# Attention beside an MLP: when sums are cleared, how many scores a phase has, and which banks they use

## The chip, the cores and the metric

The kernel runs on one core of a Trainium2 chip. The metric is the device time of one execution in microseconds (us). Before the change three runs took 1433.83, 1438.09 and 1441.65 us; the median is 1438.09 us.

## The reference

```
g = sigmoid((x * gate_w).sum(-1))
a = softmax_attention(x)            # 32 heads of 16, scores q.k * 16**-0.5, then @ wo
b = mixer(x)                        # w2^T gelu(w1^T layernorm(x) + b1) + b2, over the tokens
out = g * a + (1 - g) * b
```

x is 2048 tokens by 512 channels, w1 is 2048 x 1792, w2 is 1792 x 2048. Everything is float32; the kernel splits operands into a high and a low part and multiplies three times.

## The kernel before, in words

First come the projections to q, k and v and the first layer of the mixer (up to about 304 us). Everything after that is one schedule, written out by hand, of **phases**. A phase issues 8, 12 or 14 score matmuls; among the first of them it issues as many matmuls of other work (**beside** work), then the matmuls that multiply finished exponentials with v, then the additions. Two phases with the same beside work are a **double**: every beside matmul is split in two halves of 64 rows, one for each phase of the double, and both add to the same bank (`dn`). So that the halves never overlap, POOL writes a one-element `token` (L1152) after the last beside matmul of a phase, and the first beside matmul of the next phase (L1146) waits for it.

**Units, groups, slots, banks.** A score matmul (L990) gives one **unit**: 128 keys by 512 queries of one head, in one of seven PSUM banks. A **group** is a pair of heads with half of the queries: 64 units; there are 32 groups, 2048 units. Most units are exponentiated by ACT straight from the bank (L1020), one, two or three neighbouring banks in one instruction. Some are copied by DVE to SBUF first (L1140) and exponentiated there by ACT at the start of the next phase (L1034); now and then DVE does a whole one with a polynomial (L1046 to L1059). Every result takes a **slot** of 128x512 in SBUF: 25 in `arena` and 4 in `more`, given back when v's matmuls (L938) have read it. `matched` pairs the finished units of a group; `apply_v` multiplies them, to a bank that the phase's table names (`av_bank`, and `other_bank` for a second group); `add_sums` (L961) lets DVE add that bank to the group's sums `ot`.

The table `TURN` has, for each size of phase, the bank of every score, the scores that ACT takes together, the scores that DVE copies, and the two banks for v. For twelve:

```
12: [((0, 1, 4, 5, 6, 2, 3, 0, 1, 4, 5, 6), ((0,), (2,), (4,), (6,), (7, 8, 5), (9, 10, 11)), (1, 3), 3, 2)]
```

**Ends of groups.** When a group is complete, `store_sums` queues five transfers on SP (L884, L886), and `open_sums` of the group after next allocates `ot` (two buffers) and clears it on POOL (L874). At the end of a group's scores SP also gets 14 loads for the group after next (L515). POOL, SP, PE, ACT and DVE each run their instructions in the order in which they were queued.

**Stages.** The beside work of the first 61 doubles is the mixer's second layer (16 tiles of 42 matmuls, three doubles of 12 scores and one of 14 per tile). Then two doubles, of 14 and 8 scores, carry none; `open_end` gives the mixer's buffers to the output stage there and the four slots of `more` and one of `arena` are closed (`room`). Then 22 doubles of eight scores carry the output projection of token tiles 0 to 7 (12 matmuls each): their input comes as eight transfers a tile (`fetch_tile`, L743, L744) and is divided on DVE (L712). The last eight doubles, of eight scores, carry 8 of 12 matmuls for tiles 8 to 15; `fetch_o` (L720, L721) brings whole blocks for these. A tail finishes.

Of the kernel before, what the change touches and what calls it, by code (L numbers as in the profile page):

```python
# [10 lines left out]
F32 = mybir.dt.float32  # L11
# [11 lines left out]
P = 128  # L23
S = 2048
D = 512
# [50 lines left out]
def gated_mix(ctx: ExitStack, tc: tile.TileContext, a_x, a_wqkv, a_wo, b_w1, b_b1, b_w2, b_b2, gate_w, out):  # L76
# [3 lines left out]
    def split(hi, lo, src, copy, sub):  # L80

        copy(hi, src)  # L82
        return sub(lo, src, hi.bitcast(F32), ALU.subtract)  # L83
# [444 lines left out]
    def second_out(t, ps):  # L528
# [21 lines left out]
        ],  # L550
        12: [((0, 1, 4, 5, 6, 2, 3, 0, 1, 4, 5, 6), ((0,), (2,), (4,), (6,), (7, 8, 5), (9, 10, 11)), (1, 3), 3, 2)],
        14: [
            (
                (0, 6, 5, 1, 4, 2, 0, 6, 3, 5, 4, 1, 2, 0),
                ((0,), (2,), (3,), (5,), (8,), (10, 9, 7), (13, 11, 12)),
                (1, 4, 6),
                3,
                6,
            )
        ],  # L560
    }

# [14 lines left out]
    more_ctx = ExitStack()  # L577
    more_pool = more_ctx.enter_context(tc.tile_pool(name="more", bufs=1, reuse_waits="tile"))
    more = more_pool.tile([P, MORE, NB], F32, name="more")
    stamps = {n: 0 for n in (*range(BOX), *range(SLOTS, SLOTS + MORE))}  # L580
    room_for = [SLOTS + MORE]

    def slots(at, n):
        return arena[:, at : at + n, :] if at < SLOTS else more[:, at - SLOTS : at - SLOTS + n, :]

    def slot_of(at):
# [5 lines left out]

    def take(n, lone=False):

        room, best = room_for[0], None
        for at in range(room - n + 1):
            run = range(at, at + n)
            if not all(m in stamps for m in run):
                continue
            near = [m for b in {m // 3 for m in run} for m in range(3 * b, min(3 * b + 3, room)) if m in stamps or m in born]  # L600
            others = [born[m] for m in near if m not in stamps]
            if n == 3:
                fit = len(near) - n
            elif not others:
                fit = 2 if len(near) == 3 else 0 if lone else 1
            else:
                fit = 0 if max(others) == phase and not lone else 1 if lone else 3
            last = max(stamps[m] for m in run)
            cost = max(last, mark[0]), fit, last, at
            best = min(best, cost) if best else cost  # L610
        if best is None:
            return None
        at = best[-1]
        for m in range(at, at + n):
            del stamps[m]
            born[m] = -1 if lone else phase
        return at
# [36 lines left out]
    def whenever(phases, cost, what):  # L654
        slow.append((phase + phases, cost, what))
# [6 lines left out]
    def open_end():  # L662

        nonlocal end, wo_hi, wo_lo
        u_ctx.close()
        wk_ctx.close()
        end = end_ctx.enter_context(tc.tile_pool(name="end", bufs=1, side="right", reuse_waits="tile"))
        assert all(m in stamps for m in range(SPARE, BOX))
        assert all(m in stamps for m in range(SLOTS, SLOTS + MORE))
        more_ctx.close()  # L670
        wo_pool = end_ctx.enter_context(tc.tile_pool(name="wo", bufs=1, reuse_waits="tile"))
        wo_hi = wo_pool.tile([P, ND, D], F32R, name="wo_hi")
        wo_lo = end.tile([P, ND, D], F32R, name="wo_lo")
        for k in range(ND):
            raw = base_of(NH + k)
            nc.sync.dma_start(raw, a_wo[k * P : (k + 1) * P, :])
            parts = wo_hi[:, k, :], wo_lo[:, k, :], raw, nc.vector.tensor_copy, nc.vector.tensor_tensor
            whenever(1, 1.1, lambda parts=parts, k=k: (split(*parts), wo_done.add(k)))

        least.append(end.tile([P, 1], F32, name="least"))  # L680
        nc.vector.tensor_reduce(least[0], ident.rearrange("p (j r) -> p j r", r=32)[:, :, DH], axis=AX.X, op=ALU.add)
        nc.vector.tensor_scalar(least[0], least[0], -1.0, 3e38, ALU.add, ALU.mult)
        nc.vector.tensor_scalar_add(least[0], least[0], LEAST_SUM)
# [9 lines left out]
            )  # L693
        whenever(2, 1.9, lambda: split(wq[0], wq[1], raw, nc.vector.tensor_copy, nc.vector.tensor_tensor))

    rooms, bases = {}, {}

    def o_room(k):
        if k not in rooms:
# [1 line left out]
        return rooms[k]  # L701

    def base_of(t):
        if t not in bases:
            bases[t] = end.tile([P, D], F32, name=f"base{t}")
        return bases[t]

    def quotient(hi, lo, n):

# [88 lines left out]
    def put(steps, *shape):  # L798
        at = len(doubles)
        for n, m in shape:  # L800
            doubles.append((n, [steps.pop(0) for _ in range(m)]))
        assert not steps
        return at
# [1 line left out]
    def call(at, *what):  # L805
        calls.setdefault(at, []).append(what)

    def room(n):
        room_for[0] = n

    EARLY = 8
    AHEAD_OF_SCORES = 32
# [1 line left out]
    first = steps[:AHEAD_OF_SCORES]  # L814
    put(steps[AHEAD_OF_SCORES:], (12, 10))
    for t in range(1, NS):
        put(second_layer(t), (12, 10), (12, 10), (12, 10), (14, 12))
    call(len(doubles) - 2, room, SPARE)
    call(put([], (14, 0), (8, 0)), open_end)
    for t in range(2):  # L820
        call(len(doubles) - 2 + t, fetch_tile, t)
    for t in range(NH):
        steps, load = project(t, 3 * ND)
        at = put(steps, *([(8, 6)] * 2 if t < 2 else [(8, 4)] * 3))
        call(at - 1, load)
        if t + 2 < NH:
            call(len(doubles), fetch_tile, t + 2)
        if t in (3, 6):
            call(at, fetch_o, 1, t // 3 - 1)
    call(len(doubles) - 2, fetch_o, 1, 2)  # L830
    for t in range(NH, NS):
        steps, load = project(t, EARLY)
        call(put(steps, (8, EARLY)) - 2, load)
    call(len(doubles) - 6, room, WQ_AT)
    call(len(doubles) - 4, load_wq)
    call(len(doubles) - 2, fetch_o, 1, 3, 3)
    assert sum(n for n, _ in doubles) == NG * GROUP // 2
# [126 lines left out]
    with tc.manual_schedule(engines=engines):  # L964
# [39 lines left out]
        def exponential(units, turn, which, apart=False):  # L1004

            which = sorted(which, key=lambda m: turn[m])
            if apart and sum(m < room_for[0] for m in stamps) < len(which):
                return False
            while which:
                for n in range(len(which), 0, -1):  # L1010
                    slot = take(n)
                    if slot is not None or not apart:
                        break
                if slot is None:
                    return False
                now, which = which[:n], which[n:]
                span = [turn[m] for m in now]
                assert span == list(range(span[0], span[0] + n))
                dst = slots(slot, n)
                act = nc.scalar.activation(dst, banks[:, span[0] : span[-1] + 1, :], AF.Exp, scale=SCALE)  # L1020
                reads(act, *span)
                for at, m in enumerate(now):
                    units[m].source = act
                    hold(units[m], slot + at, phase + 1)
            return True
# [41 lines left out]
            yield result, 0.63  # L1067

        DVE_UNTIL = 18
        SPAN = {8: 3.7, 12: 5.4, 14: 6.3}  # L1070
        exp_steps, copied = [], []
        done_to, turns = 1, 0
        open_sums(0)
        open_sums(1)
        for two, (size, steps) in enumerate(doubles):
            for second in range(2):
                phase = 2 * two + second
# [18 lines left out]
                if last_phase:  # L1096

                    nc.vector.tensor_scalar_max(sums[NG - 1], sums[NG - 1], least[0])
                if size == 8:
                    turn, exps, copies, av_bank, other_bank = TURN[8][turns % 3]  # L1100
                    turns += 1
                else:
                    turn, exps, copies, av_bank, other_bank = TURN[size][0]


                mark[0] = clock[0]
                exponential_of_copies(copied)
                by_dve = copies[:1] or (1,) if not exp_steps and at[second] % (GROUP // 2) < DVE_UNTIL else ()
                for_act = [m for m in copies if m not in by_dve]
                exps = [which for which in exps if which != by_dve]  # L1110
# [49 lines left out]
                if phase == 0:  # L1160
                    shift_rows(nc.vector, k_bufs[1])

                sets = matched(phase)
                assert len(sets) <= 2
                there = []
                for (grp, pairs), bank in zip(sets, (av_bank, other_bank)):
                    while there and put_off and any(bank in [turn[m] for m in which] for which in put_off):
                        assert exponential(units, turn, put_off.pop(0), apart=True), (phase,size,len(sets),sorted(stamps),room_for,[(g,len(p)) for g,p in sets])
                    assert not any(bank in [turn[m] for m in which] for which in put_off)
                    there.append((grp, bank, apply_v(grp, pairs, bank)))  # L1170
                while put_off:
# [14 lines left out]
                for grp, bank, where in there:  # L1186
                    add_sums(grp, bank, where)
                    if summed[grp] == GROUP:
                        store_sums(grp)
                        open_sums(grp + 2)  # L1190
        assert not slow and not soon and not exp_steps and not copied

        last_ot = sums[NG - 1]
# [165 lines left out]
```

## Time and profile before

| | |
|---|---|
| median of three runs | 1438.09 us |
| profiled execution | 1433.17 us |
| its span, first to last instruction | 1431.3 us |
| granted TensorE clock over the span | 0.965 |
| busy over the span: PE, ACT, DVE, POOL | 92%, 75%, 62%, 14% |
| second-layer stage (322.8 to 1058.5 us) | 735.7 us |
| the next 58.6 us: last scores of that stage, doubles without beside work | 1058.5 to 1117.1 us |
| output projection of tiles 0 to 7 | 1117.1 to 1338.5 us |
| early projection of tiles 8 to 15 | 1338.5 to 1408.5 us |
| tail | 1408.5 to 1431.3 us |

PE is the matrix engine, PEld its weight loads, ACT the scalar engine, DVE the vector engine, POOL the general one, SP the engine that queues transfers. A row "A <- B: t, n, m" of the waits says that A's engine stood idle for t us in all, n times, m us at the longest, until B was done. In the timeline, brackets give the idle time before a row and what ended it. Each fp32 matmul for v stands as two records.

### The profile page before, as it was taken

How to read it: one execution, taken by the hardware profiler on the slowest of the kernel's cores; microseconds unless marked ns; L12 is line 12 of the kernel's file. 1: busy time of each engine (PE TensorE's matmuls, PEld its weight loads, DVE VectorE, ACT ScalarE, POOL GpSimd, SP SyncE). 2: the span in 40 equal slices, each digit the busy share in tenths (PEclk: the TensorE clock that was granted, in tenths of full speed). 3: DMA queues.
4: the chain of work that ended last, by engine and by line, in shares of the span. 5: the costliest groups of instructions: out<-in, count | busy, mean ns of one | idle time of the engine just before them, and what ended most of it. 6: DMA issues, size and time to landing. Idle time of an engine off the chain costs nothing.

```text
span 1431.3 us, 32692 instructions
## 1 busy us (share of the span) xinstructions
PE 1317.0 (92%) x13274; PEld 824.5 (58%) x13274; DVE 885.2 (62%) x1541; ACT 1080.0 (75%) x1471; POOL 203.2 (14%) x361
## 2 busy tenths in 40 slices
PE   9999999989999999999999999999987887786798
PEld 7888888855555555555555555555553444443455
DVE  5675444287776766567677576677754465564566
ACT  3453344369999999989899999998985777675784
POOL 0210444441111111111111111111100000000000
PEclk9999999989999999999999999999997988898899
DMA  3586633263332333443433333534223324344311
GB/s 126 182 304 248 193 96 96 77 147 65 65 75 54 73 73 59 81 79 61 80 72 68 66 70 63 92 68 83 50 41 95 78 73 94 79 100 104 87 38 68
DMA packets 100176, 133.17 MB, mean 93 GB/s; under 512 B 16730, under 2 KB 63984, under 8 KB 96945
## 3 DMA queue, kind: packets, MB, share of 16 engines
q1 hardware_dynamic: 99440, 129.95, 39.1%
q8 instruction: 106, 1.74, 0.6%
q10 hardware_dynamic: 576, 1.05, 0.2%
q14 instruction: 54, 0.43, 0.1%
HBM read 97.00 MB, written 33.93 MB: 91 GB/s over the span
## 4 chain that ended last, share of the span: by engine, by line
PE 65%; DMA 11%; ACT 8%; DVE 7%; SPq 6%; issue 3%; POOL 0%; POOLq 0%; DVEq 0%; ACTq 0%
PE s L938 22%; PE s L990 17%; PE acc L429 10%; PE acc L90 9%; ACT arena L1020 6%; PE dn L1146 5%; SPq L515 4%; DMA ks<-kp 3%; DMA o<-ot 3%; DVE ot L961 2%; DMA s<-ot 2%; DVE arena L1052 2%; SPq L884 1%; DMA o_hi<-r 1%; ACT more L1020 1%
## 5 line engine op out<-in xcount | busy, mean ns | idle before, releaser
L1020 ACT ACTIVATE arena<-s 128x512 f32<-128x512 f32 (+2 forms) x1029 | 778.5, 873 | 148.1 <-PE s L990 116.7
L990 PE MATMUL s<-qs,ks 64*128 64x512 f32 x2048 | 531.4, 424 | 42.7 <-DVE ot L961 22.3
L938 PE MATMUL s<-arena,v 128*17 128x256 f32 x7372 | 480.2, 388 | 5.9 <-ACT arena L1020 4.8
L990 PEld LDWEIGHTS s<-qs,ks 64*128 64x128 f32 x2048 | 337.9, 190 | 223.7 <-ACT arena L1020 58.9
L938 PEld LDWEIGHTS s<-arena,v 128*17 128x17 f32 x7372 | 211.9, 99 | 220.3 <-ACT arena L1020 52.3
L961 DVE TENSOR_TENSOR ot<-s,ot 128x256 f32<-128x256 f32 (+2 forms) x314 | 150.4, 500 | 301.1 <-PE s L938 255.6
L1146 PE MATMUL dn<-u_hi,w_hi 64*128 64x512 f32 x426 | 177.3, 416 | 4.2 <-POOL token L1152 4.2
L1146 PE MATMUL dn<-u_hi,w_lo 64*128 64x512 f32 x428 | 174.0, 407 | 5.4 <-POOL token L1152 5.4
L1146 PE MATMUL dn<-u_lo,w_hi 64*128 64x512 f32 x426 | 174.7, 410 | 4.3 <-POOL token L1152 4.3
L83 POOL TENSOR_TENSOR w_lo<-w_raw,w_hi 128x512 fp32r<-128x512 f32 (+1 forms) x126 | 152.8, 1214 | 120.0 <-ACT w_hi L82 107.8
L1052 DVE SCALAR_TENSOR_TENSOR arena<-arena 128x512 f32<-128x512 f32 x235 | 164.0, 698 | 6.3
L1140 DVE COPY arena<-s 128x512 f32<-128x512 f32 x201 | 130.6, 682 | 12.9 <-PE s L990 12.3
L1152 POOL MEMSET token<- 1x1 f32 x182 | 16.7, 92 | 674.3 <-PE dn L1146 610.1
L1034 ACT ACTIVATE arena<-arena 128x1024 f32<-128x1024 f32 (+2 forms) x100 | 112.1, 1121 | 0.0
L82 ACT CAST w_hi<-w_raw 128x512 fp32r<-128x512 f32 (+1 forms) x67 | 38.1, 569 | 79.7 <-PE acc L429 58.7
L938 PE MATMUL s<-more,v 128*17 128x256 f32 x820 | 92.6, 382 | 1.6 <-ACT arena L1020 1.6
L1020 ACT ACTIVATE more<-s 128x512 f32<-128x512 f32 (+2 forms) x93 | 84.9, 947 | 8.9 <-PE s L990 8.8
L429 PE MATMUL acc<-h_hi,w_hi 128*128 128x512 f32 x224 | 87.1, 389 | 0.0
L429 PE MATMUL acc<-h_hi,w_lo 128*128 128x512 f32 x224 | 87.1, 389 | 0.0
L429 PE MATMUL acc<-h_lo,w_hi 128*128 128x512 f32 x224 | 87.1, 389 | 0.0
L1146 PEld LDWEIGHTS dn<-u_hi,w_lo 64*128 64x128 f32 x428 | 80.0, 187 | 9.5 <-POOL token L1152 7.0
L1146 PEld LDWEIGHTS dn<-u_lo,w_hi 64*128 64x128 f32 x426 | 79.4, 186 | 7.9 <-POOL token L1152 5.9
(155 smaller groups left out, 1481.6 us busy)
## 6 DMA issues: line engine op xcount, KB each, us to landing
w_raw<-in_B_w_dram SPq DMA_DIRECT2D x96, 256.0 KB
ks<-kp SPq DMA_DIRECT2D x192, 128.0 KB
qs<-qp SPq DMA_DIRECT2D x256, 64.0 KB
qp<-pc SPq DMA_DIRECT2D x16, 768.0 KB
x<-in_A_x_dram SPq DMA_DIRECT2D x32, 256.0 KB
kp<-pc SPq DMA_DIRECT2D x16, 512.0 KB
w_raw<-in_B_w_dram SPq DMA_DIRECT2D x32, 128.0 KB
bp<-row SPq DMA_DIRECT2D x16, 256.0 KB
```

What stands on the lines that cost most here:

```text
L83: return sub(lo, src, hi.bitcast(F32), ALU.subtract)
L90: nc.tensor.matmul(ps, a, b, start=start and n == 0, stop=stop and n == last)
L429: nc.tensor.matmul(p, a, b, start=first and k == 0, stop=last and k == 2)
L515: nc.sync.dma_start(dst[at].bitcast(F32), src[b][part[which], rows, cols])
L938: mm = nc.tensor.matmul(av[32 * j : 32 * j + VC, u.i * QC : (u.i + 1) * QC], v[:, u.c, g % NP * 2 + u.i, :], u.p[:, h * QC : (h + 1) * QC] ...
L961: reads(nc.vector.tensor_tensor(x, y, x, ALU.add), bank)
L990: mm = nc.tensor.matmul(banks[:, bank, :], kt[grp][rows, c * P : (c + 1) * P], qt[grp][rows, qb * NB : (qb + 1) * NB], start=True, stop=True,)
L1020: act = nc.scalar.activation(dst, banks[:, span[0] : span[-1] + 1, :], AF.Exp, scale=SCALE)
L1034: act = nc.scalar.activation(dst, dst, AF.Exp, scale=SCALE)
L1052: nc.vector.scalar_tensor_tensor(box[1], box[1] if q is None else q, a, x, ALU.add, ALU.mult)
L1140: ins = nc.vector.tensor_copy(slot_of(slot), bank)
L1146: mm = nc.tensor.matmul(ps, a[half], b[half], start=first_of and not second, stop=last_of and bool(second))
```

## The change

- `open_sums` of a group is called at the start of the first phase after the group's first scores, no longer when the group two before it is stored.
- `matched` is called ahead of the phase's scores, so that the table can have another order of banks for phases with two groups.
- Phases of 14 are gone. The second layer takes doubles of 12 scores throughout: nine of its tiles take four doubles with 8 beside matmuls and one with 10, the other six take four with 10, 12, 10 and 10. The two doubles without beside work and the output projections of tiles 0 to 7 have 12 scores, the latter 12 beside matmuls. The last eight doubles stay as they are.
- Slots are closed one by one (`shut_slots`) and not by a limit; the eight `base` buffers of the end (L705) become one tile, which serves as slots until its parts are needed.

```diff
-        12: [((0, 1, 4, 5, 6, 2, 3, 0, 1, 4, 5, 6), ((0,), (2,), (4,), (6,), (7, 8, 5), (9, 10, 11)), (1, 3), 3, 2)],
-        14: [
-            (
-                (0, 6, 5, 1, 4, 2, 0, 6, 3, 5, 4, 1, 2, 0),
-                ((0,), (2,), (3,), (5,), (8,), (10, 9, 7), (13, 11, 12)),
-                (1, 4, 6),
-                3,
-                6,
-            )
+        12: [
+            ((4, 2, 5, 0, 1, 6, 4, 3, 5, 2, 0, 1), ((0,), (2,), (4,), (5,), (6, 8, 7), (10, 11, 9)), (1, 3), 6, 2),
+            ((1, 4, 5, 0, 2, 6, 3, 4, 5, 1, 2, 0), ((0,), (2,), (3,), (6,), (7, 8, 5), (9, 11, 10)), (1, 4), 3, 6),
         ],
...
+    BASES = 33
     stamps = {n: 0 for n in (*range(BOX), *range(SLOTS, SLOTS + MORE))}
-    room_for = [SLOTS + MORE]
+    shut = set()
+    bases = []
 
     def slots(at, n):
+        if at >= BASES:
+            return bases[0][:, at - BASES : at - BASES + n, :]
...
     def take(n, lone=False):
 
-        room, best = room_for[0], None
-        for at in range(room - n + 1):
+        free, best = {m for m in stamps if m not in shut}, None
+        for at in free:
             run = range(at, at + n)
-            if not all(m in stamps for m in run):
+            if not free.issuperset(run) or (lone and at >= SLOTS):
                 continue
...
+        bases.append(end.tile([P, NH, D], F32, name="bases"))
+        open_slots(*range(BASES + ND, BASES + NH))
         for k in range(ND):
             raw = base_of(NH + k)
             nc.sync.dma_start(raw, a_wo[k * P : (k + 1) * P, :])
             parts = wo_hi[:, k, :], wo_lo[:, k, :], raw, nc.vector.tensor_copy, nc.vector.tensor_tensor
-            whenever(1, 1.1, lambda parts=parts, k=k: (split(*parts), wo_done.add(k)))
+            whenever(1, 1.1, lambda parts=parts, k=k: (split(*parts), wo_done.add(k), open_slots(BASES + k)))
...
-        put(second_layer(t), (12, 10), (12, 10), (12, 10), (14, 12))
-    call(len(doubles) - 2, room, SPARE)
-    call(put([], (14, 0), (8, 0)), open_end)
+        put(second_layer(t), *([(12, 8)] * 4 if t * 3 // 5 > (t - 1) * 3 // 5 else [(12, 10), (12, 12), (12, 10)]), (12, 10))
+    call(len(doubles) - 1, shut_slots, SPARE, *range(SLOTS, SLOTS + MORE))
+    call(put([], (12, 0), (12, 0)), open_end)
...
         steps, load = project(t, 3 * ND)
-        at = put(steps, *([(8, 6)] * 2 if t < 2 else [(8, 4)] * 3))
+        at = put(steps, (12, 12))
...
         steps, load = project(t, EARLY)
-        call(put(steps, (8, EARLY)) - 2, load)
-    call(len(doubles) - 6, room, WQ_AT)
+        at = put(steps, (8, EARLY))
+        call(at - 3, shut_slots, BASES + t - NH)
+        call(at - 2, load)
+    call(len(doubles) - 6, shut_slots, *range(WQ_AT, SPARE))
...
-        open_sums(0)
-        open_sums(1)
+        opened = 0
...
+                mark[0] = clock[0]
+                if max(at) > GROUP // 2 * opened:
+                    open_sums(opened)
+                    opened += 1
+                exponential_of_copies(copied)
+                sets = matched(phase)
+                assert len(sets) <= 2
                 if size == 8:
                     turn, exps, copies, av_bank, other_bank = TURN[8][turns % 3]
                     turns += 1
                 else:
-                    turn, exps, copies, av_bank, other_bank = TURN[size][0]
-
-
-                mark[0] = clock[0]
-                exponential_of_copies(copied)
+                    turn, exps, copies, av_bank, other_bank = TURN[size][len(sets) > 1]
...
-                sets = matched(phase)
-                assert len(sets) <= 2
                 there = []
...
                     if summed[grp] == GROUP:
                         store_sums(grp)
-                        open_sums(grp + 2)
```

More of the change, by code (lines that the diff above doesn't have):

```diff
@@ L593, in take @@
     def take(n, lone=False):
-        room, best = room_for[0], None
-        for at in range(room - n + 1):
+        free, best = {m for m in stamps if m not in shut}, None
+        for at in free:
             run = range(at, at + n)
-            if not all(m in stamps for m in run):
+            if not free.issuperset(run) or (lone and at >= SLOTS):
                 continue
-            near = [m for b in {m // 3 for m in run} for m in range(3 * b, min(3 * b + 3, room)) if m in stamps or m in born]
-            others = [born[m] for m in near if m not in stamps]
+            near = [m for b in {m // 3 for m in run} for m in range(3 * b, 3 * b + 3) if m in free or m in born and m not in stamps]
+            others = [born[m] for m in near if m not in free]
             if n == 3:
@@ L694, in load_wq @@
         whenever(2, 1.9, lambda: split(wq[0], wq[1], raw, nc.vector.tensor_copy, nc.vector.tensor_tensor))
-    rooms, bases = {}, {}
+    rooms = {}
     def o_room(k):
@@ L703, in base_of @@
     def base_of(t):
-        if t not in bases:
-            bases[t] = end.tile([P, D], F32, name=f"base{t}")
-        return bases[t]
+        at = BASES + t - NH
+        assert at not in stamps or at in shut
+        return slot_of(at)
     def quotient(hi, lo, n):
@@ L806, in call, with shut_slots, open_slots @@
         calls.setdefault(at, []).append(what)
-    def room(n):
-        room_for[0] = n
+    def shut_slots(*which):
+        shut.update(which)
+    def open_slots(*which):
+        stamps.update((m, clock[0]) for m in which)
     EARLY = 8
@@ L1006, in exponential @@
             which = sorted(which, key=lambda m: turn[m])
-            if apart and sum(m < room_for[0] for m in stamps) < len(which):
+            if apart and sum(m not in shut for m in stamps) < len(which):
                 return False
@@ L1069, in gated_mix @@
         DVE_UNTIL = 18
-        SPAN = {8: 3.7, 12: 5.4, 14: 6.3}
+        SPAN = {8: 3.7, 12: 5.4}
         exp_steps, copied = [], []
         done_to, turns = 1, 0
-        open_sums(0)
-        open_sums(1)
+        opened = 0
         for two, (size, steps) in enumerate(doubles):
@@ L1167, in gated_mix @@
                     while there and put_off and any(bank in [turn[m] for m in which] for which in put_off):
-                        assert exponential(units, turn, put_off.pop(0), apart=True), (phase,size,len(sets),sorted(stamps),room_for,[(g,len(p)) for g,p in sets])
+                        assert exponential(units, turn, put_off.pop(0), apart=True)
                     assert not any(bank in [turn[m] for m in which] for which in put_off)
```

## The prediction

> **What bounds the kernel now.** I read the page first, then the busy time by windows cut where the code changes its stage, then the list of waits for each window, then the chain of waits and the timeline around the longest of them.
>
> ```profile
> span 1431.3 us, 32692 instructions
> PE 1317.0 (92%) x13274; PEld 824.5 (58%) x13274; DVE 885.2 (62%) x1541; ACT 1080.0 (75%) x1471; POOL 203.2 (14%) x361
> ```
>
> The page calls PE busy for 92%, which would leave little to win by moving waits about. The stages say otherwise. In the next rows the columns are the stretch, its length, then busy time and count of PE, PEld, DVE, ACT and POOL, the granted clock, DMA share and GB/s. The stretches are the first two phases of scores, the second-layer stage, the bridge to the output stage, its part with whole projections and its part with early projections; the tail, 1408.5 to the end, is 22.8 us. The last row is the score matmuls alone, with their count (PE, PEld).
>
> ```profile
> 304.30:322.80 18.50, 11.83 (x86) 6.26 (x86) 15.43 (x21) 11.27 (x14) 2.83 (x5) 0.72 0.68 149
> 322.80:1058.50 735.70, 703.99 (x8600) 406.33 (x8596) 500.79 (x881) 682.62 (x903) 90.00 (x197) 1.00 0.37 70
> 1058.50:1117.10 58.60, 42.92 (x404) 22.07 (x400) 27.50 (x50) 33.88 (x44) 1.25 (x5) 0.80 0.29 71
> 1117.10:1338.50 221.40, 177.31 (x1966) 95.16 (x1962) 122.60 (x207) 163.74 (x211) 6.20 (x49) 0.88 0.38 83
> 1338.50:1408.50 70.00, 62.14 (x724) 35.29 (x720) 43.45 (x79) 56.30 (x72) 3.19 (x17) 0.93 0.26 62
> 322.80:1058.50 735.70, 374.69 (x1472) 241.22 (x1472) 1.00 0.37 70
> ```
>
> The second-layer stage is full: PE 96%, ACT 93%, clock 1.00, 735.7/1472 = 0.500 us per score unit. The bridge has ACT at 58%, the output stage at 74%, both at a lower clock: 58.6/72 = 0.81 and 221.4/352 = 0.63 us per unit (72 and 352 by the code). What is lost there shows in the chain of waits around the longest gap:
>
> ```profile
> 1148.23 1.74 DMA s<-ot
> ...
> 1150.25 0.02 POOL ot L874
> ...
> 1150.71 0.10 POOL token L1152
> ...
> 1150.85 0.79 PE dn L1146
> ...
> 1151.65 0.42 PE dn L1146
> ```
>
> The last units of a group are added; SP stores its sums; the memset that clears the buffer for the group after next (L874) stands on POOL right behind and waits until the stores have landed. The token (L1152) stands behind that memset on POOL, and the next phase's first beside matmul waits for the token, with all later scores behind it in PE's order. The lists of waits give the price (total us, times, longest): whole run, then second-layer stage, whole projections, early projections; and what POOL itself waited for.
>
> ```profile
> PE dn L1146 <- POOL token L1152: 56.2, 18, 9.7
> PE dn L1146 <- POOL token L1152: 11.8, 11, 2.8
> PE dn L1146 <- POOL token L1152: 35.0, 5, 9.7
> PE dn L1146 <- POOL token L1152: 7.3, 1, 7.3
> POOL ot L874 <- DMA s<-ot: 160.4, 16, 14.8
> PE s L990 <- DVE ot L961: 12.4, 19, 1.3
> ```
>
> **The change, part by part.** Working rates first, from the chain (PE) and the timeline (ACT; brackets are the idle time before and its releaser).
>
> ```profile
> 336.94 3.20 PE s L938 x56
> 340.15 0.43 PE s L990
> 340.58 0.23 PE s L990
> 1069.10 2.79 ACT L1020 ACTIVATE arena<-s 128x1536 f32<-128x1536 f32 x2 [4.79 <-PE s L938]
> 1079.63 2.79 ACT L1020 ACTIVATE arena<-s 128x1536 f32<-128x1536 f32 x2 [3.46 <-PE s L938]
> 1082.30 1.49 ACT L1034 ACTIVATE arena<-arena 128x1536 f32<-128x1536 f32 x1
> 1083.68 2.56 ACT L1020 ACTIVATE arena<-s 128x512 f32<-128x512 f32 x5
> 1091.97 2.79 ACT L1020 ACTIVATE arena<-s 128x1536 f32<-128x1536 f32 x2 [5.73 <-PE s L938]
> 1102.38 1.45 ACT L1020 ACTIVATE arena<-s 128x1536 f32<-128x1536 f32 x1 [3.81 <-PE s L938]
> ```
>
> PE: two half-array matmuls every 0.23 us; a v record takes 3.20/56 = 0.057 us, and a unit has four: of the 8600 PE records of the second-layer stage 1472 are scores and 1236 beside work by the code (90 phases of ten, 28 of twelve), (8600-1472-1236)/1472 = 4.0. ACT, start to start: two triples 1082.30-1079.63 = 2.67; five singles in 2.56, so 0.48 each when the last one's drain is taken off; three copies from the arena 1083.68-1082.30 = 1.38, so a pair about 0.95. A phase of twelve is four singles, two triples and one pair: 1.92+2.67+0.95 = 5.55 us of ACT. On PE it is (12+10)/2 x 0.23 + 48 x 0.057 = 5.27, and I add 0.35: the first score after v takes 0.43 and not 0.23, and the last ones drain (0.15, my estimate). The two are even; neither can hide much of the other.
>
> *Sums cleared at the group's first scores.* The memset moves some three phases behind the stores (a group of 64 units lasts 5.3 phases of twelve, its stores go out one to two phases after its last score), over 15 us after stores whose longest wait shown is 14.8. POOL then waits for nothing, the token is early, and the 56.2 us go. What is late next is the bank of the added sums and ACT's order, which the rates above include. Each long gap has a tail as well: after the 9.7 us the first beside matmul takes 0.79 and the next 0.42 us, not the 0.23 of a full clock, and the granted clock of these stages is 0.88 and 0.93. I take ten steps at 0.2 more, 2 us a gap; six gaps in the two output stages (5 and 1 in the lists), 12 us.
>
> The Trainium skill (TensorE: Matmul & The Clock Gate, "A second HAM failure mode: psum-queue depth-cycling") says that cycling through PSUM banks makes PE idle briefly between groups of matmuls, so often that its clock swings between half and full rate. That rule speaks against more phases of one cycled order; by it alone the new phases would not gain the clock back. This trace disagrees in the second-layer stage, which cycles seven banks at a granted 1.00. The sum goes by the row.
>
> *Matching ahead of the scores.* It moves no instruction; it lets the order be chosen by the number of groups. At nothing.
>
> *Bank order.* With one group, v's sums now sit in the bank of score 5 (6 before), so the next phase needs DVE's add one score earlier: 0.23 us where that wait exists, 19 phases in the waits above, 4 us; it costs 138 x 0.23 = 32 us at worst, and below nothing down to minus the 12.4 us of that wait, since v's bank is also freed one single sooner. I take +4, nearest to the row. Score 1 now sits in a bank that the previous phase's last triple empties (score 2 before); PE needs 5.6 us per phase and ACT 5.55, so PE comes there after the triple's end: nothing, unless PE runs ahead.
>
> *Twelve everywhere.* The second-layer stage becomes 69 doubles, 138 phases, 1656 units, with 1260 beside half-matmuls: 9.1 a phase, against 10.5 before. At the old rate without token waits: (735.7-11.8)/1472 x 1656 = 814; less 1.4 x 0.117 us per phase where PE is last (half the phases): -11; with the +4, 807. Ends: 138 x 5.55 = 766 and 0.500 x 1656 = 828.
>
> *The bridge.* Before, four phases of fourteen ran with 24 free slots; two triples each waited until v's matmuls gave slots back: 4.79+3.46+5.73+3.81 = 17.8 us of idle ACT. After, two phases of twelve have 24 slots, then four phases without beside work have 28 and soon 32. Twelve held and twelve needed fit only just, so I leave one triple late in each of the two: 7 us (0 to 17.8). The four: 4 x 5.55 + 2 = 24.
>
> *Whole projections at (12, 12).* Sixteen phases: PE 12 x 0.23 + 2.74 + 0.35 = 5.85, ACT 5.55: 94 us. On top, the tile fetch. Its rows in the timeline: SP's first and last issue, then DVE's wait and division; SP's loads of a new group; and DVE's longest wait for a fetch of a whole block.
>
> ```profile
> 1159.17 0.38 SPq L743 DMA_DIRECT2D o_lo<-o  x1
> ...
> 1163.04 0.59 SPq L744 DMA_DIRECT2D o_hi<-r  x1
> ```
> ```profile
> 1166.06 0.69 DVE L712 TENSOR_TENSOR arena<-o_lo,o_hi 128x512 f32<-128x512 f32 x1 [1.10 <-DMA o_hi<-r]
> 1167.25 0.69 DVE L83 TENSOR_TENSOR o_lo<-arena,o_hi 128x512 fp32r<-128x512 f32 x1
> ```
> ```profile
> 1132.81 4.44 SPq L515 DMA_DIRECT2D qs<-qp  x8
> 1137.29 2.73 SPq L515 DMA_DIRECT2D ks<-kp  x6
> ```
> ```profile
> 1290.40 0.69 DVE L712 TENSOR_TENSOR arena<-o_lo,o_hi 128x512 f32<-128x512 f32 x1 [3.98 <-DMA o_hi<-r]
> ```
>
> From first issue to divided tile: 1167.94-1159.17 = 8.8 us, inside a double of 11.7. With a group's fourteen loads ahead on SP (7.2 us) it is 16.0, 4.3 late, and DVE's adds wait behind the division. That falls on three of eight doubles, one of them with a block fetch (3.98): some 12 us in place of the like waits of before. 94+12 = 106 (94 to 140).
>
> *Early projections.* Same shape; 70.0 less the 7.3 and its 2 us tail: 60.
>
> **The sum** on the profiled execution: 322.8 (up to the second phase) + 807 + 7 + 24 + 106 + 60 + 22.8 (tail) = 1349.6, and 1.9 outside the span (1433.17 beside 1431.3): 1351.5. The median of the runs, 1438.09, lies 4.9 above the profiled one, so 1356.
>
> **The rivals** (times on the median's scale).
>
> *The fetch becomes the bound.* If every double of the whole projections, not three, ends as late as the loads make it, DVE blocks PE eight times: 8 x 4.3 and two block fetches at 3.98, 42 less the 12 taken, 30 more: 1386. For it: SP issues in order, and t's tile is fetched only one double ahead. Against: SP's 14 loads come once per 64 units, and 192 units pass.
>
> *ACT's floor.* With PE relieved of 1.4 halves a phase the second-layer stage runs at ACT's 766: 41 less, 1315. For: 5.55 against 5.5 of PE. Against: this stage never held it so far (0.500 x 12 = 6.0).
>
> *The memset still waits.* If the stores land late because SP has fetches ahead of them, POOL blocks as before: 56.2+12 back, 1424. Against: three phases of room.
>
> *The bank order costs a wait each phase.* Score 1 finds its bank in use, PE stands until the last triple ends, half a triple (0.67 us) each: 158 phases x 0.67 = 106: 1462, slower. It decides from (1438-1356)/158 = 0.52 us per phase. Against: PE arrives last by the rates above.
>
> *The clock swings.* If the gaps at the banks push the second-layer stage to the output stage's 0.88, 807/0.88 = 917: 1466. The rule of the Trainium skill quoted above would have it so; the 1.00 of the long stage is against it.
>
> **How the numbers follow.** Forecast 0.67, fetch 0.11, ACT's floor 0.08, memset 0.06, bank order 0.06, clock 0.02. Range 1312 to 1408: it takes in the floor and the fetch case and, above, the end of the second-layer term with the fetch's (+21, +30); it leaves out the last three, 0.14. A difference of 0.5% is about what a measurement of this kernel can tell. The first three are all faster; of the memset case a third may end within 0.5%: faster 0.90, same 0.02, slower 0.08.
>
> **What would show it.** Right: no PE wait for the token above 1 us, POOL's memset with no DMA as releaser; granted clock near 1.0 in the whole projections; the second-layer stage at 0.47 to 0.50 us per unit; ACT's waits for v in the bridge under 8 us. Wrong: score matmuls waiting for ACT in every phase, DVE's division waiting for o_hi for over 20 us in all, or token waits that stay.

## The result, and the profile after

The changed kernel takes 1360.34 us (four runs, 1360.06 to 1360.98), the kernel before 1437.53 us beside it: a ratio of 0.9463, 95% interval 0.9437 to 0.9489. The forecast was 1356.

The page of the changed kernel begins with

```profile
span 1359.2 us, 32545 instructions
PE 1296.9 (95%) x13274; PEld 810.4 (60%) x13274; DVE 909.1 (67%) x1546; ACT 1077.0 (79%) x1429; POOL 217.9 (16%) x351
```

PE has the same instructions, and ACT's busy time is unchanged within 3 us. Of the 72 us of span, PE's idle time gave 52 (114.3 before, 62.3 now) and its busy time 20: the granted clock over the span is 0.982, not 0.965. By windows, cut again at the changes of stage (long stage, bridge, whole projections, early projections, tail; busy time and count of PE, PEld, DVE, ACT, POOL, then clock, DMA share, GB/s). The long stage is the one with the second layer:

```profile
325.10:1122.90 797.80, 780.63 (x9546) 440.64 (x9542) 572.85 (x956) 764.25 (x973) 109.25 (x222) 1.00 0.36 68
1122.90:1150.20 27.30, 22.84 (x246) 10.46 (x242) 20.35 (x40) 22.45 (x29) 0.00 (x0) 0.94 0.66 148
1150.20:1271.80 121.60, 100.47 (x1156) 58.88 (x1152) 78.36 (x139) 90.47 (x114) 3.00 (x19) 0.89 0.55 125
1271.80:1336.00 64.20, 61.32 (x748) 34.33 (x744) 46.71 (x87) 56.15 (x72) 3.72 (x18) 1.00 0.29 67
1336.00:1359.20 23.20, 16.54 (x164) 11.44 (x160) 11.86 (x24) 5.43 (x9) 1.37 (x2) 0.92 0.26 95
```

The long stage now holds 1656 units at 797.8/1656 = 0.482 us (0.500 before), PE 98% and ACT 96% busy. The bridge is half as long, with 48 units instead of 72: 0.57 us per unit, not 0.81. Only the whole projections are still loose, with a clock of 0.89 and the same 0.63 us per unit as before (121.6/192). The lists of waits of the whole run, for PE, DVE and the longest of POOL:

```profile
PE s L995 <- DVE ot L966: 28.0, 27, 6.3
PE dn L1153 <- DVE o_hi L82: 8.2, 2, 4.2
DVE arena L712 <- DMA o_hi<-r: 21.3, 5, 5.8
POOL token L1159 <- PE dn L1153: 861.9, 167, 34.3
```

PE's 56.2 us of waits for the token are gone; POOL has no wait for a store left, it idles until PE's next beside matmul. What is left is PE waiting for DVE: 9.5 of the 28.0 us are spread over the long stage, and 20 us of the two rows lie in two phases of the whole projections, 9.6 and 10.4. The chain through the first:

```profile
1191.40 0.42 SPq L515
...
1191.87 6.20 DMA ks<-kp
...
1198.09 0.59 SPq L744
...
1198.72 0.46 SPq L720
...
1199.23 8.81 DMA o_hi<-r
...
1208.15 0.70 DVE arena L712
...
1209.34 0.69 DVE o_lo L83
1210.03 0.34 DVE ot L966
...
1210.42 0.79 PE s L995
...
1211.22 0.42 PE s L995
```

Beside it, SP's loads of a group and the first transfer of the tile, and DVE's two divisions:

```profile
1184.88 4.63 SPq L515 DMA_DIRECT2D qs<-qp  x8
1189.55 2.73 SPq L515 DMA_DIRECT2D ks<-kp  x6
1192.33 0.42 SPq L743 DMA_DIRECT2D o_lo<-o  x1
1201.31 0.69 DVE L712 TENSOR_TENSOR arena<-o_lo,o_hi 128x512 f32<-128x512 f32 x1 [4.83 <-DMA o_hi<-r]
1208.15 0.69 DVE L712 TENSOR_TENSOR arena<-o_lo,o_hi 128x512 f32<-128x512 f32 x1 [4.96 <-DMA o_hi<-r]
```

A group's loads go out first, then a tile's eight transfers (L743, L744), then a block fetch (L720, L721), whose second transfer lands 8.8 us after its issue. The eight transfers are themselves stretched: they are issued from 1192.33 to 1198.68, 6.4 us, against 4.5 where no loads stand ahead (1159.17 to 1163.63, with the prediction), and in the chain the last of them starts when the group's last load has landed. DVE stands at the tile's division, then at the block's; the addition that frees a bank stands behind that, and the scores behind the addition. Then PE's matmuls come every 0.42 us and not every 0.23. That phase takes 19.5 us, its like two doubles and a half later 19.3, where the ordinary one takes about 5.8.

### The profile page after: what moved, and what is told of

Read it like the earlier page. It is cut to its first block, busy times and chain, and to the rows that moved or that the text cites. A ratio compares the mean times of both kernels' runs of the same rounds, so it can differ in the third digit from the quotient of the medians.

```text
span 1359.2 us, 32545 instructions
## 1 busy us (share of the span) xinstructions
PE 1296.9 (95%) x13274; PEld 810.4 (60%) x13274; DVE 909.1 (67%) x1546; ACT 1077.0 (79%) x1429; POOL 217.9 (16%) x351
## 4 chain that ended last, share of the span: by engine, by line
PE 75%; DVE 10%; ACT 7%; DMA 4%; SPq 2%; issue 1%; DVEq 0%; ACTq 0%
PE s L943 27%; PE s L995 24%; PE acc L429 11%; PE acc L90 9%; ACT arena L1025 6%; DVE arena L1057 2%; PE dn L1153 2%; DVE ot L966 2%; DMA o_hi<-r 2%; SPq L515 1%; DMA ks<-kp 1%; DVE arena L1147 1%; ACT more L1025 1%; DVE arena L1061 1%; DVE arena L1064 1%
## 5 line engine op out<-in xcount | busy, mean ns | idle before, releaser
L1025 ACT ACTIVATE arena<-s 128x512 f32<-128x512 f32 (+2 forms) x899 | 721.2, 901 | 70.8 <-PE s L995 43.1
L995 PE MATMUL s<-qs,ks 64*128 64x512 f32 x2048 | 519.4, 419 | 39.1 <-DVE ot L966 28.0
L995 PEld LDWEIGHTS s<-qs,ks 64*128 64x128 f32 x2048 | 324.5, 186 | 233.8 <-DVE ot L966 50.2
L943 PE MATMUL s<-arena,v 128*17 128x256 f32 x6996 | 455.0, 383 | 5.4 <-ACT arena L1025 3.2
L943 PEld LDWEIGHTS s<-arena,v 128*17 128x17 f32 x6996 | 202.6, 98 | 194.2 <-ACT arena L1025 38.9
L966 DVE TENSOR_TENSOR ot<-s,ot 128x512 f32<-128x512 f32 (+2 forms) x271 | 134.0, 522 | 233.6 <-PE s L943 211.1
L1057 DVE SCALAR_TENSOR_TENSOR arena<-arena 128x512 f32<-128x512 f32 x265 | 193.7, 731 | 7.2
L1147 DVE COPY arena<-s 128x512 f32<-128x512 f32 x215 | 139.4, 680 | 1.1 <-PE s L995 0.4
L1039 ACT ACTIVATE arena<-arena 128x1024 f32<-128x1024 f32 (+1 forms) x121 | 121.7, 1006 | 0.0
L1025 ACT ACTIVATE more<-s 128x512 f32<-128x512 f32 (+1 forms) x111 | 98.8, 931 | 10.3 <-PE dn L1153 6.0
```

Of the source, the lines that this page charges most:

```text
L943: mm = nc.tensor.matmul(av[32 * j : 32 * j + VC, u.i * QC : (u.i + 1) * QC], v[:, u.c, g % NP * 2 + u.i, :], u.p[:, h * QC : (h + 1) * QC] ...
L966: reads(nc.vector.tensor_tensor(x, y, x, ALU.add), bank)
L995: mm = nc.tensor.matmul(banks[:, bank, :], kt[grp][rows, c * P : (c + 1) * P], qt[grp][rows, qb * NB : (qb + 1) * NB], start=True, stop=True,)
L1039: act = nc.scalar.activation(dst, dst, AF.Exp, scale=SCALE)
L1057: nc.vector.scalar_tensor_tensor(box[1], box[1] if q is None else q, a, x, ALU.add, ALU.mult)
L1147: ins = nc.vector.tensor_copy(slot_of(slot), bank)
```

## The experiments

All ratios are against the kernel before on the same chip. Beside the several kernels its median lay between 1434.9 and 1437.5 us, so a difference of two medians is good to about 3 us. Rows called "alone" and "sums and loads behind" vary the kernel before, the others the changed one. Stage lengths are of the profiled execution, cut as above (us):

| kernel | median | ratio, interval | long | bridge | whole | early |
|---|---|---|---|---|---|---|
| before | 1437.5 | | 735.7 | 58.6 | 221.4 | 70.0 |
| changed | 1360.3 | 0.946 (0.944-0.949) | 797.8 | 27.3 | 121.6 | 64.2 |
| sums as before | 1410.8 | 0.983 (0.981-0.986) | 840.9 | 25.8 | 131.5 | 65.1 |
| sums alone | 1401.3 | 0.977 (0.976-0.979) | 725.7 | 54.9 | 210.9 | 60.5 |
| old banks | 1361.1 | 0.949 (0.947-0.951) | 799.1 | 28.0 | 119.7 | 63.9 |
| loads behind | 1350.5 | 0.942 (0.940-0.943) | 797.9 | 23.4 | 115.5 | 64.2 |
| output in eights | 1368.6 | 0.953 (0.951-0.955) | 706.9 | 40.3 | 212.4 | 60.4 |
| no base slots | 1375.2 | 0.957 (0.956-0.959) | 797.8 | 29.1 | 134.3 | 65.3 |
| sums and loads behind | 1383.8 | 0.963 (0.961-0.965) | 725.5 | 55.2 | 193.8 | 60.5 |
| loads behind, blocks early | 1336.6 | 0.931 (0.929-0.932) | 797.8 | 23.4 | 105.5 | 62.0 |
| fourteens again | 1383.4 | 0.964 (0.960-0.967) | 747.6 | 110.3 | 112.7 | 63.4 |
| both tiles early | 1331.1 | 0.927 (0.924-0.930) | 798.0 | 23.4 | 98.9 | 61.9 |
| loads behind alone | 1430.1 | 0.995 (0.993-0.997) | 728.9 | 58.3 | 225.2 | 67.7 |

The long stage has 1656 units in the changed kernel and its variants, but 1472 in before and its variants, 1440 with the output in eights, 1500 with fourteens again.

**The sums.** First the changed kernel with the old place, then the old kernel with the new place.

```diff
-                if max(at) > GROUP // 2 * opened:
-                    open_sums(opened)
-                    opened += 1
...
                         store_sums(grp)
+                        open_sums(grp + 2)
```

> The changed kernel with the sums cleared as before (when the group two earlier is stored). If the memset's wait was the price of the stalls: POOL waits for the stores again, PE for the token in some 18 places, 45 to 68 us in all, 1405 to 1428 us. Rival, that phases of twelve hide the stores anyway: under 1370 us, with token waits under 10 us in all.

1410.75: as expected, 50 us more than the changed kernel. Its long stage in the windows, then PE's waits in the whole run and in that stage:

```profile
323.30:1164.20 840.90, 795.59 (x9544) 453.53 (x9540) 561.75 (x957) 767.31 (x973) 99.57 (x221) 0.98 0.35 65
PE dn L1151 <- POOL token L1157: 50.1, 21, 18.8
PE dn L1151 <- POOL token L1157: 30.3, 18, 3.1
```

But 43 of the 50 us lie in the long stage, where before showed 11.8 us of token waits and where moving the sums alone gave 10 (735.7 to 725.7). In this schedule the same memset stops PE there 18 times, 30.3 us in all, and slows it as well: the same matmuls keep PE busy for 795.6 us, not 780.6, as the granted clock falls from 1.00 to 0.98. PE's idle time grows by 28.1 us and its busy time by 15.0; together these are the 43. Why 18 of the group ends meet the next phase's token here, and only 11 in the old schedule, I didn't settle. The Trainium skill (TensorE: Matmul & The Clock Gate, "A second HAM failure mode: psum-queue depth-cycling") tells of a kernel whose PE idles briefly between groups of matmuls as it cycles through the banks, so often that its clock swings. The runs agree only this far: 18 stops of up to 3.1 us go with a clock two hundredths lower, while the kernel before had 11 of up to 2.8 us at 1.00, and cycling seven banks without such stops holds 1.00 over 800 us.

> The kernel before with nothing changed but the place where sums are cleared. By the prediction's sum the 56 us of token waits and 12 us of slow clock go: about 1370 us (1365 to 1380). Rival, that the next late thing (the tile fetch, DVE's adds) takes the place of the token: 1400 us or more, with new waits of PE for DVE in the output stage.

1401.27: the rival's. The token waits are gone, and half of their price has come back under another name. Its whole projections, and the waits of the whole run; the last row is of the kernel before:

```profile
1103.50:1314.40 210.90, 174.36 (x1964) 91.89 (x1960) 124.31 (x207) 163.24 (x211) 6.68 (x49) 0.90 0.40 87
PE s L990 <- DVE ot L961: 50.0, 38, 9.7
DVE arena L712 <- DMA o_hi<-r: 26.4, 9, 8.2
DVE arena L712 <- DMA o<-ot: 18.5, 2, 9.8
```

PE's wait for added sums went from 22.3 us (whole run; the 12.4 with the prediction is of the long stage) to 50.0, and the whole projections gave only 10 us where the list had promised 35. The token had stood on top of a late fetch, and the trace of before had it: DVE's division (L712), which reads the fetched tile, stood 9.5 us under o_hi and 18.5 more, in two places, under the stores of a group's sums. The longer of these, 9.8 us, ends at 1148.55, 2.3 us before the token lets PE go on at 1150.85; there SP issues the stores right behind the tile's transfers. With the sums moved it is 26.4 and 10.1 us: DVE's waits grew by 8.5, but PE's wait for DVE by 27.7.

**What the fetches stand behind.** In these kernels the loads of q and k for the group after next are queued on SP after the fetches of the same phase.

```diff
-                while min(at) >= GROUP // 2 * done_to:
-                    if done_to + 1 < NG:
-                        qt[done_to + 1] = load_q(done_to + 1)
-                        kt[done_to + 1] = load_k(done_to + 1)
-                    done_to += 1
...
                 if not second:
                     for what, *args in calls.get(two, ()):
                         what(*args)
                     beside = [step(*args) for step, *args in steps]
+                while min(at) >= GROUP // 2 * done_to:
+                    if done_to + 1 < NG:
+                        qt[done_to + 1] = load_q(done_to + 1)
+                        kt[done_to + 1] = load_k(done_to + 1)
+                    done_to += 1
```

> The changed kernel with SP's fourteen loads of the next group's q and k queued behind the tile and block fetches of the same phase, not ahead. If the two phases of 19 us in the output stage come from the fetches standing behind the loads: 7 us less in each, about 1346 us. Rival, that the block transfer itself (8.8 us to landing) is what DVE waits for: within 3 us of 1360.

1350.47, 10 us less (14 expected). The first long phase falls from 19.5 to 11.1 us, the second from 19.3 to 10.3, but the first phase of the stage grows from 7.3 to 12.7. The Trainium skill (DMA: Bandwidth & Descriptors, "Issuing engines are not separate DMA queues") holds the time to initiate a transfer to be usually small beside the transfer. For one transfer the trace agrees: a load takes 0.42 us to issue, and the last of a group lands 6.20 us after its issue begins. It is the sum that delays: the fourteen loads, one behind another, hold SP for 7.2 us ahead of the fetch, in rows shown with the prediction.

> The kernel before with nothing changed but SP's loads behind the fetches of the same phase. If the token wait and the late fetch lie over one another at the same places, either alone brings less than its list says: with the token still waiting for the stores, which stay behind the loads, within 8 us of before. Rival, that the two add up: 15 us or more faster than before, as between the kernels with the sums moved.

1430.14, 7 us. Where the token still waits, an earlier fetch is worth little:

```profile
PE dn L1146 <- POOL token L1152: 50.8, 14, 11.4
```

The 7 us are not in the whole projections, which take 225.2 us (221.4 before), with 38.0 us of token waits (35.0 before). In the long stage the token waits fall from 11.8 to 4.7 us.

> The kernel before with the sums cleared at the group's first scores and SP's loads behind the fetches of the same phase. The sums alone gave 34 us of the 68 expected. If the tile fetches, late behind the group's loads, took the token's place: most of the missing 34 us comes here, 1370 to 1382 us, and DVE's waits for o_hi fall under 15 us. Rival, that the token waits were hiding other work and only half was ever to be had: 1395 us or more.

1383.77, just outside the expected stretch: 17.5 us less than the sums alone, about half of the 34 that were missing. Sums 34, loads 7, both 53: the two waits lie over one another. In the whole projections alone, the sums gave 10.5 us, the loads none, both 27.6. DVE's waits for o_hi are not under 15 us:

```profile
DVE arena L712 <- DMA o_hi<-r: 16.9, 7, 4.9
PE s L990 <- DVE ot L961: 36.1, 38, 6.2
```

**Banks, phases, slots.** The old order of banks for both entries of twelve:

```diff
-            ((4, 2, 5, 0, 1, 6, 4, 3, 5, 2, 0, 1), ((0,), (2,), (4,), (5,), (6, 8, 7), (10, 11, 9)), (1, 3), 6, 2),
-            ((1, 4, 5, 0, 2, 6, 3, 4, 5, 1, 2, 0), ((0,), (2,), (3,), (6,), (7, 8, 5), (9, 11, 10)), (1, 4), 3, 6),
+            ((0, 1, 4, 5, 6, 2, 3, 0, 1, 4, 5, 6), ((0,), (2,), (4,), (6,), (7, 8, 5), (9, 10, 11)), (1, 3), 3, 2),
+            ((0, 1, 4, 5, 6, 2, 3, 0, 1, 4, 5, 6), ((0,), (2,), (4,), (6,), (7, 8, 5), (9, 10, 11)), (1, 3), 3, 2),
```

> The changed kernel with the bank order of before for phases of twelve, for one group and for two. If the order is worth little, as predicted (+4 us against the new one): 1352 to 1365 us. Rival, that the new order is what keeps PE from waiting at the banks: 1375 us or more, with more waits of scores for ACT or DVE in the second-layer stage.

1361.10: the order is worth nothing that can be measured. In the long stage scores wait for added sums 6.6 us with the old order (9 times) and 9.5 with the new one (17 times), which is the direction of the prediction's +4; v's matmuls wait for ACT's arena 5.5 us against 3.2 and give it back. The first row of each pair is of the old order:

```profile
PE s L995 <- DVE ot L966: 6.6, 9, 1.1
PE s L995 <- DVE ot L966: 9.5, 17, 1.4
PE s L943 <- ACT arena L1025: 5.5, 10, 0.7
PE s L943 <- ACT arena L1025: 3.2, 6, 0.7
```

The output stage in eights:

```diff
-        put(second_layer(t), *([(12, 8)] * 4 if t * 3 // 5 > (t - 1) * 3 // 5 else [(12, 10), (12, 12), (12, 10)]), (12, 10))
+        put(second_layer(t), (12, 10), (12, 10), (12, 10), (12, 12))
-    call(put([], (12, 0), (12, 0)), open_end)
+    call(put([], (12, 0), (12, 0), (12, 0)), open_end)
-        at = put(steps, (12, 12))
+        at = put(steps, (8, 4), (8, 4), (8, 4))
```

> The changed kernel with the whole projections in phases of eight scores (three doubles of 8 scores and 4 beside matmuls a tile); the second layer then takes 60 doubles of 12 with 10, 10, 10 and 12 beside matmuls, and one more double without beside work. If the fetches' lateness and not the size of the phases sets the output stage: 96 more units there at about the same price as in the long stage, 1350 to 1370 us. Rival, that small phases cost by themselves what before showed (0.53 us per unit without token waits, against 0.48): 1375 us or more.

1368.63, 8 us slower than the changed kernel. It lies in the first theory's stretch, near its end. The 216 units that leave the long stage save 90.9 us there, 0.421 us each; 192 of them cost 90.8 us in the output stage, 0.473 each, and the other 24 cost 13.0 in the bridge; the early projections are 3.8 shorter. So the changed kernel wins by having those units beside the second layer, where its unit costs 0.482 us against 706.9/1440 = 0.491. That twelve scores a phase win anything in the output stage itself is not shown, since a tile here also has six phases for its fetch instead of two, and DVE still waits 19.8 us for o_hi.

Phases of fourteen again, with the beside work as before:

```diff
-        put(second_layer(t), *([(12, 8)] * 4 if t * 3 // 5 > (t - 1) * 3 // 5 else [(12, 10), (12, 12), (12, 10)]), (12, 10))
+        put(second_layer(t), (12, 10), (12, 10), (12, 10), (14, 12))
+    put([], *[(14, 0)] * 3, *[(12, 0)] * 3)
```

> The changed kernel with the second layer's doubles as before (three of 12 and one of 14 scores a tile, 10, 10, 10 and 12 beside matmuls) and the 156 units that this leaves over in six doubles more without beside work, ahead of the closing of the slots. If the long stage is bound by PE's sum of work, it matters little where beside work lies: the long stage at the 0.493 us per unit that the sums alone gave, 726 us, and the 156 units at ACT's 0.46, 72 us, 798 in all as in the changed kernel: 1355 to 1367 us. Rival, that phases of fourteen cost by themselves (banks, slots): 1372 us or more.

1383.42, the rival's: the long stage and the 156 moved units take 747.6+87.7 = 835.3 us. The expected 798 was summed wrongly: the long stage has 1500 units here, not the 1472 that 726 stands for, and the first theory gives 0.493 x 1500 + 72 = 811, some 1374 us for the whole kernel, which is on the rival's side of the line. So the line does not divide the two; what is left to explain is the 24 us by which 835.3 lies above 811. In its windows these are

```profile
324.20:1071.80 747.60, 716.96 (x8758) 413.33 (x8754) 525.45 (x899) 696.85 (x932) 97.66 (x202) 1.00 0.37 69
1071.80:1159.50 87.70, 73.79 (x801) 35.07 (x797) 54.21 (x89) 72.46 (x100) 1.05 (x2) 0.96 0.27 50
```

The long stage costs 0.498 us per unit; against the 0.491 of twelves with the same beside work, fourteens cost 0.007. The units without beside work cost 0.562, far above the 0.46 that ACT's work alone makes, with ACT 83% busy. What the rival named is there, at both places. Banks: over nearly the whole long stage PE waits longer for added sums than in the kernel with the sums alone, which has the same phases and the old order of banks (second row).

```profile
PE s L999 <- DVE ot L970: 18.5, 32, 1.4
PE s L990 <- DVE ot L961: 12.0, 19, 1.3
```

Slots: of ACT's 15.2 us of idle time in the units without beside work, 11.1, in four places, end with v's matmuls, as the triples that lacked slots did in the bridge before; three of the four lie in its first 50 us, where the phases of fourteen are. That is 6.5 and 11.1 of the 24 us; I did not follow the rest. Against the changed kernel there is also where beside work lies: the same beside matmuls, spread thinly over more phases, keep both PE and ACT near full.

Without the slots in the bases:

```diff
-        open_slots(*range(BASES + ND, BASES + NH))
-            whenever(1, 1.1, lambda parts=parts, k=k: (split(*parts), wo_done.add(k), open_slots(BASES + k)))
+            whenever(1, 1.1, lambda parts=parts, k=k: (split(*parts), wo_done.add(k)))
```

> The changed kernel without the eight base buffers as slots: from the last double of the second layer on there are 24. If slots bind with phases of twelve as they did with fourteen (a triple late, some 2 us in each of 20 phases): about 1400 us, ACT waiting for v's matmuls. Rival, that 24 slots are enough for twelve scores: under 1366 us.

1375.19: between the two, 15 us slower. ACT waits for v's matmuls for slots as expected, but in 11 places, not 20 (bridge and most of the output stage; the changed kernel has no such row there):

```profile
ACT arena L1024 <- PE s L942: 26.1, 11, 3.6
```

**Two steps further.** With the loads behind, the first two block fetches moved to tiles whose doubles have no group loads, and divided a phase later:

```diff
-            whenever(2 if n < P // DH else 1, 1.75, lambda i=i: divide(i))
+            whenever(2, 1.75, lambda i=i: divide(i))
-        if t in (3, 6):
-            call(at, fetch_o, 1, t // 3 - 1)
+        if t in (2, 4):
+            call(at, fetch_o, 1, t // 2 - 1)
```

> The changed kernel with SP's loads behind the fetches, the first two block fetches moved to tiles 2 and 4 (from 3 and 6), and their divisions due one phase later. If the two 19 us phases are a late fetch that DVE's adds stand behind, this takes most of the 27 us above an ordinary phase: 1332 to 1343 us. Rival, that the transfers themselves are short of time in the output stage: no better than the loads alone, 1347 to 1353 us.

1336.56, as expected. One long phase is left at the start of the stage, 12.8 us; there tile 1's fetch stands behind a group's loads and stores. So it goes out with tile 0's:

```diff
-        call(len(doubles) - 2 + t, fetch_tile, t)
+        call(len(doubles) - 2, fetch_tile, t)
```

> The kernel with loads behind and blocks early, and the fetch of tile 1 issued with that of tile 0, one double sooner. If the 12.8 us first phase of the output stage there is tile 1's fetch standing behind a group's loads and stores: 6 to 8 us less than that kernel, 1329 to 1332 us. Rival, that DVE then has too much to do ahead of it (weights' splits and two divisions): 1335 us or more.

1331.13 us, as expected: 29 us faster than the changed kernel, ratio 0.9266 (0.9235 to 0.9297) to the kernel before. Its whole projections:

```profile
1146.00:1244.90 98.90, 95.69 (x1158) 56.78 (x1154) 78.86 (x139) 90.28 (x114) 3.28 (x19) 0.98 0.64 146
```

98.9 us at a clock of 0.98, against the 94 that the prediction had for this stage without any late fetch. So what the stage had lost came from the fetches' place in SP's and DVE's order, and not from the transfers.

## Why the prediction was right, and where its steps were not

- *The token's chain* was read rightly: the sums' place takes every token wait away, in both kernels. **The price was not the list.** The prediction took 56.2 us and 12 of slow clock and held that what is late next was in its rates already. Alone the step gives 34 us, since in the output stage a late tile fetch lay under the token's wait; in the changed schedule it gives 50, mostly in the long stage, where before had shown 11.8. The sum hardly rests on this price: it takes most stages at working rates, and from the list only 11.8 us for the long stage and 9.3 for the early projections, where the sums alone gave 10.0 and 9.5.
- *The long stage*: 807 forecast, 797.8 measured. The relief from beside work was taken for half of the phases, 11 us; for all of them it is 138 x 1.4 x 0.117 = 23, and 814 - 23 = 791. With PE 98% busy the stage came near that. The rival of ACT's floor, 766, was not reached. The +4 for the bank of score 5 is there as waits, 2.9 us, and is given back elsewhere.
- *Score 1 behind the last triple* and *the swinging clock*, the two slower rivals: in the long stage PE waits 1.3 us for banks that ACT empties, and the clock is 1.00.
- *The bridge*: 31 forecast, 7 for two late triples and 24 for the four phases; 27.3 measured. The triples were not late: ACT waits for no matmul of v, there or in the long stage. With the loads behind the fetches the bridge takes 23.4 us, so the four phases cost what was summed, and the 3.9 above it are a late fetch once more. The slots in the bases carry 15 us over bridge and output stage.
- *Whole projections*: 106 forecast, 121.6 measured, the term that was mis-sized. An ordinary phase takes about 5.8 us, as summed (5.85). The mechanism of the late fetch was named, and so was the mark by which the prediction would be wrong, over 20 us of DVE's waits for o_hi: they are 21.3. What it missed is that tile and block fetch come in one phase behind the same loads, so DVE waits twice (4.83, then 4.96 us), PE stops, and the clock falls: 13.6 us above an ordinary phase, two times, 27 and not 12. The forecast of a clock near 1.0 there was wrong with it (0.89); it is 0.98 where the fetches come in time.
- *Early projections* 60 against 64.2, of which 2.2 go when the blocks are fetched earlier; the start 322.8 against 325.1; the tail 22.8 against 23.2. In all +9.6 on the span: -9.2 (long) -3.7 (bridge) +15.6 (whole) +4.2 (early) +2.7 (start and tail). That the forecast of 1356 is only 4 us off is partly luck: stages too high and too low cancel, and the 4.9 us added because the median before lay above its profiled run had no counterpart after (1360.34 beside 1360.98).

## What to carry to other kernels

A list of waits gives what a wait costs while nothing else is late underneath it. Before summing such a list, ask for each place which transfer or engine would have been next, and when it was ready; and read an instruction's idle time under all of its releasers, since the late division stood mostly under another name than o_hi. An instruction that only tidies up (a memset of a buffer used much later) must not stand in an in-order queue ahead of one on which another engine's next step depends; nor a load needed in 30 us ahead of one needed in 10. In this kernel, work that fills an engine's gaps was best spread so that each phase has both engines full.

## What was not expected of the hardware

- 18 stops of PE of up to 3.1 us in the long stage came with a granted clock of 0.98 and cost 43 us: 28 of idle time and 15 of slower matmuls. 11 stops of up to 2.8 us had left it at 1.00.
- Of a block fetch's two transfers of 512 KB the second landed 8.8 us after its issue, with a tile's transfers in flight.
